# A cosine fold of w_in put ahead of the first product, and three matmuls on ones between two products, in a fused Fourier-mixing and gated-cosine kernel

## The chip, the cores and the metric

The kernel runs on one core of one Trainium2 chip. The metric is the device time of one execution in microseconds (us). The kernel before: a median of 1924.36 us in 3 runs (1923.04 to 1927.86) when the prediction was made. Each run also comes with TensorE's mean granted clock.

## The reference, cut to what matters

```python
def _attn_ref(x):                      # x: (8, 3008, 256) float32
    X = np.fft.fft(x, axis=1)
    X = np.fft.fft(X, axis=2)
    return X.real.astype(np.float32)

def _moe_ref(x, w_in, w_out):          # x: (24064, 256), w_in: (256, 2048), w_out: (2048, 256)
    h = x @ w_in
    g = h * np.cos(h)
    return (g @ w_out).astype(np.float32)
```

The second runs on the output of the first. The kernel doesn't compute the channel transform by itself: it folds the cosine and sine matrices of that transform into `w_in`, once, in its opening, and keeps the results as `Wc` and `Ws`. `w_in` comes in four quarters; a fold is a pair of matmuls for one quarter and one of the two matrices.

## The kernel before

The parts that the change touches. A fold fills a PSUM bank, and a copy on the scalar engine (ScalarE, ACT in the profile) takes it from there to `Wc` or `Ws`:

```python
def fold_mms(q, part, tag):
    ps = bank(tag)
    for h in range(2):
        mm(ps, CC[:, h * 256 + part : h * 256 + part + 128], w1[q][:, h], h == 0, h == 1)
    return ps
...
def fold_copy(q, ri):
    act((Ws if ri else Wc)[:, q * 512 : (q + 1) * 512], pending.pop((q, ri)))
```

The first spectrum's imaginary part is made from short matmuls on 95 and 94 rows into banks pB and M, a copy of pB to `ab`, and two vector ops into the ring `Ir`, both of which read bank M:

```python
def early(self, te, to):
    self.uv, self.pb = bank(te), bank(to)      # first_I: pB and M
    self.mms(0, self.uv, True)
    self.mms(1, self.pb, True)
...
def plus(self):      # Ir <- ab + M
def minus(self):     # Ir <- M - ab, the mirrored half
```

The kernel starts with matmuls on a tile of ones, to lift the clock:

```python
def warm(n):
    w = bank("M")
    for _ in range(n):
        mm(w, ones[:, 0:128], ones[:, 128:640], True)
```

Order on each engine is set by a list of pairs of a time and a function, sorted by the time (`T` is the length of a step); the times are an order, not a clock. Banks such as M exist once, so whoever takes one anew waits for its last reader.

## Time and profile before

| | before |
|---|---|
| profiled run | 1928.04 us, span (first to last instruction) 1926.1 us, mean clock 0.997 |
| TensorE busy | 99% of the span |
| first product `H<-Rr` | starts at 32.31 us, after 1.86 us of idle TensorE |
| clock at half | 32.9 to 43.1 us |
| first product of the second layer, `pA<-G` | starts at 51.35 us |

The body from there on is TensorE's nearly alone, so what counts is when TensorE gets into it. The prediction below shows the windows and TensorE's timeline. What makes the idle gap is seen in the chain that ended last, in order of time (start, duration, what):

```profile
25.53 5.66 DMA wex<-wl
...
31.27 0.48 ACT H L310
31.78 0.48 ACT H L310
32.27 0.04 issue
32.31 1.52 PE H L298 x4
```

A transfer of one row of turned weights (`wex`) takes 5.66 us, two copies into bank H follow, and the first product adds to that bank. TensorE has nothing ordered to do meanwhile.

### The profile page before, as it was taken

How to read it: one execution, taken by the hardware profiler on the slowest of the kernel's cores; microseconds unless marked ns; L12 is line 12 of the kernel's file. 1: busy time of each engine (PE TensorE's matmuls, PEld its weight loads, DVE VectorE, ACT ScalarE, POOL GpSimd, SP SyncE). 2: the span in 40 equal slices, each digit the busy share in tenths (PEclk: the TensorE clock that was granted, in tenths of full speed). 3: DMA queues.
4: the chain of work that ended last, by engine and by line, in shares of the span. 5: the costliest groups of instructions: out<-in, count | busy, mean ns of one | idle time of the engine just before them, and what ended most of it. 6: DMA issues, size and time to landing. Idle time of an engine off the chain costs nothing.

```text
span 1926.1 us, 28934 instructions
## 1 busy us (share of the span) xinstructions
PE 1908.7 (99%) x9007; PEld 1655.0 (86%) x9008; DVE 1451.3 (75%) x2364; ACT 1519.5 (79%) x2994; POOL 1521.6 (79%) x2045
## 2 busy tenths in 40 slices
PE   8999999999999999999999999999999999999998
PEld 5888888888888888888888888888888888888887
DVE  6898877777777777777777777777777777777777
ACT  3778788878878887888788787888878887877886
POOL 5788888998888888888889898888888676655554
PEclk8999999999999999999999999999999999999999
DMA  9623311322023122311232113311122110100101
GB/s 201 39 66 70 66 33 28 64 34 59 16 56 49 42 43 37 62 33 35 49 60 33 41 24 60 52 43 32 27 30 36 20 21 16 17 12 12 22 10 25
DMA packets 259969, 80.58 MB, mean 42 GB/s; under 512 B 240393, under 2 KB 243256, under 8 KB 259816
## 3 DMA queue, kind: packets, MB, share of 16 engines
q1 hardware_dynamic: 248456, 48.65, 15.5%
q0 software_dynamic: 9184, 29.83, 8.5%
q8 instruction: 72, 1.18, 0.3%
q14 instruction: 81, 0.66, 0.1%
q10 hardware_dynamic: 2176, 0.26, 0.1%
HBM read 36.72 MB, written 24.69 MB: 32 GB/s over the span
## 4 chain that ended last, share of the span: by engine, by line
PE 89%; ACT 4%; DVE 3%; issue 1%; POOL 1%; DMA 0%; POOLq 0%; DVEq 0%; ACTq 0%
PE H L298 35%; PE pC L298 16%; PE pD L298 16%; PE pB L298 15%; PE pA L298 8%; ACT G L310 1%; DVE G L840 1%; DVE G L304 1%; ACT E L310 1%; ACT z L310 1%; ACT M L310 1%; DVE v L304 1%; ACT H L310 0%; DVE M L304 0%; POOL xl L182 0%
## 5 line engine op out<-in xcount | busy, mean ns | idle before, releaser
L307 POOL TENSOR_TENSOR G<-G 128x256 f32<-128x256 f32 x1500 | 1084.4, 734 | 354.9 <-DVE G L840 278.8
L840 DVE SCALAR_TENSOR_TENSOR G<-H,G 128x512 f32<-128x512 f32 x376 | 259.1, 689 | 219.2 <-ACT G L310 218.6
L304 DVE TENSOR_TENSOR G<-H,G 128x512 f32<-128x512 f32 x376 | 259.6, 690 | 215.0 <-ACT G L310 211.7
L298 PE MATMUL H<-Ir,Ws 127*128 127x256 f32 x1504 | 388.6, 380 | 3.0 <-ACT E L310 2.3
L298 PE MATMUL H<-Rr,Wc 128*128 128x256 f32 x1504 | 388.6, 381 | 2.8 <-ACT H L310 2.8
L298 PE MATMUL pC<-G,WT 128*128 128x256 f32 x1504 | 387.5, 380 | 0.7 <-DVE u L304 0.7
L310 ACT ACTIVATE H<-Rb,wex 128x256 f32<-128x256 f32 x752 | 359.9, 479 | 24.1 <-DVE G L840 9.8
L310 ACT ACTIVATE G<-H 128x512 int32<-128x512 f32 x376 | 223.8, 595 | 179.7 <-DVE G L304 178.7
L310 ACT ACTIVATE E<-H 128x512 f32<-128x512 f32 x376 | 223.9, 595 | 163.1 <-PE H L298 161.6
L298 PEld LDWEIGHTS H<-Ir,Ws 127*128 127x128 f32 x1504 | 284.0, 190 | 47.7 <-ACT E L310 6.1
L298 PEld LDWEIGHTS pC<-G,WT 128*128 128x128 f32 x1504 | 285.2, 190 | 42.7 <-PE H L298 1.5
L298 PEld LDWEIGHTS H<-Rr,Wc 128*128 128x128 f32 x1504 | 281.3, 190 | 43.8 <-ACT H L310 5.4
L310 ACT ACTIVATE G<-G,halfpi 128x512 f32<-128x512 f32 x376 | 269.3, 716 | 2.3 <-DVE G L304 2.2
L304 DVE TENSOR_TENSOR G<-E,H 128x512 f32<-128x512 f32 x376 | 255.2, 679 | 6.1 <-PE H L298 6.1
L304 DVE TENSOR_TENSOR M<-G,M 128x512 f32<-128x512 f32 x376 | 257.6, 685 | 0.0
L840 DVE SCALAR_TENSOR_TENSOR G<-G,M 128x512 f32<-128x512 f32 x376 | 254.3, 676 | 0.5 <-ACT M L310 0.5
L310 ACT ACTIVATE M<-M,halfpi 128x512 f32<-128x512 f32 x376 | 245.6, 653 | 0.0
L298 PE MATMUL pB<-G,WT 128*128 128x256 f32 x752 | 224.7, 380 | 0.2 <-POOL G L307 0.2
L298 PE MATMUL pA<-G,w 128*128 128x256 f32 x752 | 223.9, 379 | 0.0
L310 ACT ACTIVATE M<-G 128x512 int32<-128x512 f32 x376 | 223.7, 595 | 0.0
L298 PE MATMUL pD<-G,WT 128*128 128x256 f32 x752 | 223.7, 379 | 0.0
L298 PE MATMUL pB<-G,w 128*128 128x256 f32 x752 | 223.7, 379 | 0.0
(164 smaller groups left out, 2068.3 us busy)
## 6 DMA issues: line engine op xcount, KB each, us to landing
out_dram<-ot SPq DMA_DIRECT2D x496, 32.0 KB
xl<-in_x_dram SPq DMA_DIRECT2D x64, 192.0 KB
e<-e POOLq DMA_DIRECT2D x22, 384.0 KB, 5.0
o<-o POOLq DMA_DIRECT2D x22, 381.0 KB, 4.9
out_dram<-ot SPq DMA_DIRECT2D x256, 2.0 KB
Rb<-r SPq DMA_DIRECT2D x10, 376.0 KB
w<-in_moe_w_in_dram SPq DMA_DIRECT2D x4, 512.0 KB
out_dram<-ot SPq DMA_DIRECT2D x64, 28.0 KB
```

The lines of the kernel that those rows point to most:

```text
L298: nc.tensor.matmul(out_, lhsT=lhsT, rhs=rhs, start=start, stop=stop, skip_group_check=True)
L304: pin(nc.vector.tensor_tensor(out=o, in0=a, in1=b, op=op))
L307: pin(nc.gpsimd.tensor_tensor(out=o, in0=a, in1=b, op=op))
L310: pin(nc.scalar.activation(out=o, in_=i, func=func, **kw))
L840: nc.vector.scalar_tensor_tensor(out=o, in0=h, scalar=TWO_PI, in1=c, op0=ALU.mult, op1=ALU.mult)
```

## The change

It puts a fold that doesn't depend on that transfer into the gap, moves its copy forward too, and puts three matmuls on all 128 rows of ones ahead of the second product, where TensorE waits for `Ir`. The intent is to keep TensorE's clock up.

```diff
         (0.97, first_I.copy_e),
+        (1.5, lambda: warm(3)),
         (1.0, first_I.plus),
         (1.05, first_I.minus),
-        (2.3, lambda: fold_mm(1, 0, "pD")),
+        (-0.05, lambda: fold_mm(1, 0, "pD")),
         (T + 0.5, lambda: fold_mm(2, 1)),
-        (T + 0.87, lambda: fold_copy(1, 0)),
+        (0.3, lambda: fold_copy(1, 0)),
```

## The prediction

> **What bounds the kernel now.** I read the page first (the busy shares and the clock row of the 40 slices), then the windows view over the stretches of the trace, then TensorE's timeline from 28 to 64 us, the waits, and the order of the compiled instructions with their semaphores.
>
> ```profile
> PE 1908.7 (99%) x9007; PEld 1655.0 (86%) x9008; DVE 1451.3 (75%) x2364; ACT 1519.5 (79%) x2994; POOL 1521.6 (79%) x2045
> PEclk8999999999999999999999999999999999999999
> ```
>
> TensorE is busy 99% of the span, and the windows view gives it 1796.4 of the 1800 us between 100 and 1900 us. So the body is TensorE's, and the change, which touches only the opening, can win only time by which TensorE enters the body earlier. The leading 8 of the clock row says that the clock was below full in the first 48 us slice. The windows (columns: stretch, its length, TensorE busy, granted clock, DMA share, GB/s) say where:
>
> ```profile
> 26.10:29.52 3.42, 3.42 (x22) 1.00 1.07 283
> 29.52:32.93 3.41, 1.54 (x6) 1.00 1.08 394
> 32.93:36.34 3.41, 3.41 (x15) 0.50 1.10 233
> 36.34:39.76 3.42, 2.71 (x8) 0.50 1.61 70
> 39.76:43.17 3.41, 3.41 (x6) 0.50 1.80 4
> ```
>
> The clock falls to half at about 32.9 us and comes back at about 43.1 us: 10.2 us at half speed, after a window in which TensorE was busy only 1.54 us. In the timeline:
>
> ```profile
> 28.56 1.88 PE L298 MATMUL H<-w,CC 128*128 128x512 f32 x4
> 32.31 1.52 PE L298 MATMUL H<-Rr,Wc 128*128 128x256 f32 x4 [1.86 <-ACT H L310]
> ...
> 36.53 1.52 PE L298 MATMUL M<-MC,z 94*128 94x188 f32 x4
> 38.76 2.08 PE L298 MATMUL H<-Ir,Ws 127*128 127x256 f32 x4 [0.71 <-DVE Ir L304]
> 40.62 3.14 PE L298 MATMUL pD<-w,CC 128*128 128x512 f32 x4
> 43.60 1.03 PE L298 MATMUL H<-Rr,Wc 128*128 128x256 f32 x4
> ```
>
> The reader is to see an idle gap of 1.86 us before the first product (it waits for ScalarE's copy into H, which waits for a small transfer), and that the same four-matmul group takes 1.52 and 2.08 us in the slow stretch against 1.03 us from 43.60 on, and the pD fold 3.14 us against the 1.88 us of the same form at 28.56.
>
> **What the Trainium skill says.** (1) "TensorE: Matmul & The Clock Gate", Part 1, "What's actually happening": the gate passes half or all of the pulses, decided over a free-running window of 3413 ns that doesn't restart with the kernel. The trace agrees: 32.93 to 43.1 is three such windows, and counting back from it by that window meets about 5.6 us, where the trace's first row of back-to-back opening matmuls begins to run fast (71 of them in 17.47 us). (2) The same page, "Why this matters for your kernels", allows idle gaps up to about 3 us. This trace differs: 1.86 us was enough. And 3.41 us of unbroken work on 95 rows (32.93 to 36.34) did not lift the clock, which the page doesn't mention. (3) The same page, "Architectural detail", says ScalarE and VectorE are strict FIFOs; I use that for the new place of the copy, and the timeline's order on ScalarE agrees with program order. (4) "Back-to-back issue gap" gives N/2.4 + 2.5 ns, 216 ns for 512 columns; the opening's warm bf16 matmuls took 13.26/62 = 0.214 us.
>
> **The change part by part.** The order of instructions shows three differences on TensorE and one on ScalarE; vector engine, GpSimd and the transfers keep theirs.
>
> *The fold moved forward.* Its four matmul records now stand between the fold into H at 28.56 and the first product. They need only weights that the fold before them already used. At full clock each is 0.43 us, so 1.72 us, from 30.3 to 32.0, in the gap of 1.86 us: no delay for the first product at 32.31. The window 29.52 to 32.93 is then some nine tenths busy, so the clock stays up. From 32.31: the product 0.87 us, then 16 short matmuls. The same 16 forms ran at full clock from 26.28 to 28.56, 2.28 us, so they end at 35.5 instead of 38.05. Removed from its old place, the fold saves 2.94 us (40.83 to 43.77 in the chain).
>
> *The copy moved forward.* On ScalarE it takes 0.53 us ahead of E and ab: Wc 33.93, E 34.46, ab 34.99 to 35.48. That just meets TensorE's 35.5, so the vector engine's first Ir op starts at 35.65 (38.15 before); it and the second end at 36.65.
>
> *The three matmuls on ones.* They write bank M, which the short matmuls filled and which both Ir ops read; the order shows that their weight load waits for the vector engine and that the product after them doesn't any more. So the product, which before started 0.06 us after the first Ir op, now starts after the second (+0.46 us) and after 3 x 0.214 = 0.64 us of ones: about 37.4, ending 38.4, against 38.76 and 40.83.
>
> *Sum.* H<-Ir ends 2.4 us earlier; the next H<-Rr starts at 38.3 instead of 43.77, 5.4 us earlier. But not all of that is kept. The elementwise chain starts 2.4 us earlier; ScalarE has one op (0.55 us) fewer to do there; and its wait of 1.12 us for TensorE ahead of Ws goes. Following ScalarE's queue by the durations of the rows, the copies into H for the third product end at 43.8, those for the fourth at 51.1 instead of 55.13. I take 4.1 us for the gain at this point. The wex transfer lands at 34.20 + 7.4 = 41.6, before it is wanted. From there on I see the same work shifted, and the later idle bits (1.66 us from 60 to 100) are waits between engines that shift along. Gain in the case of the profile: 4.1 us.
>
> **The rivals.** (A) *The fall of the clock is a matter of phase.* The windows run free, so whether the gap of 1.86 us falls into one window or into two differs between executions. The times before are 1923.04, 1924.36, 1927.86 and, for the profiled run, 1928.04: two pairs about 4.2 us apart, as if two had kept the clock and two had lost it, the profiled one surely having lost it. Then the change brings only the slow pair down: 1928.0 - 4.1 = 1923.9. Against the fast pair it costs: without the fall, H<-Ir would start at 36.25, so the ones and their wait add 1.1 to 1.2 us, of which the ScalarE op removed later gives back 0.55: 1923.7 + 0.6 = 1924.3. For it: the even split at the size of the gain; against it: four numbers are few, and other jitter may make them. (B) *Every run before loses the clock*, and the spread is other jitter: then the change takes 4.1 us from the median, 1920.3. (C) *The changed kernel still loses the clock.* Between 35.5 and 36.7 TensorE is idle for 1.2 us, and the 2.3 us before it are matmuls on 95 rows. If the monitor counts rows, a window around these holds about as little as the one that failed. In the trace's phase it ends at 36.34 with some 0.8 us of idle time. The clock would then halve for a window of dense work, at a loss of 1 to 2 us, in perhaps a quarter of the runs. (D) *A late transfer takes over*: the last two weight quarters or wex not landed when TensorE comes earlier. The traffic drops from 233 to 70 GB/s by 36 to 40 us, so the quarters have landed; wex has 2 us of slack. It would cost up to 2 us; I give it 5%.
>
> **Range and chances.** A at 65% gives about 1924.0, B at 25% gives 1920.3, C and D add up to 2 us to either in some runs. Weighted: 0.65 x 1924.0 + 0.25 x 1920.3 + 0.10 x 1925.5 = 1923.2. The range 1920.6 to 1925.7 leaves one tenth on each side. Two per cent is 38 us, nine times the largest effect found here, and the change adds under 2 us of work: faster 0.005, within 0.99, slower 0.005.
>
> **What would show it.** In the changed profile: pD<-w at 30.3 us within the gap; clock 1.00 from 5 us on with no half-speed stretch; pB and M groups ending near 35.5; three M<-ones at about 36.7, waiting for the vector engine's Ir; H<-Ir at about 37.4 and H<-Rr at 38.3; the first pA<-G at 46 to 47 us instead of 51.35; fast runs closer together than the 4.8 us of before. Wrong would be: a half clock again after 36 us (C); the pA group at 50 us or later, or idle stretches from 50 to 100 us that grow by as much as the opening gained; a spread as wide as before, which would deny that the clock's phase makes it.

## More of the kernel before

A step `i` of the body has two products into one bank H (`H<-Rr,Wc`, then `H<-Ir,Ws`), with a doubled copy E of the first taken between them, so the second product waits for E:

```python
def dbl(i):
    S.E = spool.tile([128, 512], FP, tag="E", bufs=2, name="E")
    act(S.E, S.H, scale=2.0)
```

## The result

| | before | after |
|---|---|---|
| median, us | 1924.22 (4 runs, 1923.04 to 1927.86) | 1924.39 (4 runs, 1924.13 to 1925.19) |
| ratio | | 0.9998, 95% interval 0.9981 to 1.0016 |
| profiled run, us | 1928.04, clock 0.997 | 1924.51, clock 0.999 |
| mean clock of the timed runs | (listed only in the later runs) | 0.999 in all four |

A ratio here is taken over the runs of both kernels, those that lost the clock (below) included, so it isn't quite the ratio of the medians. The profiled runs differ by 3.5 us, and the runs after lie within 1.1 us where those before spread over 4.8 us.

The changed kernel's page, the busy shares and the clock of the 40 slices:

```profile
PE 1905.5 (99%) x9011; PEld 1652.4 (86%) x9011; DVE 1451.9 (76%) x2364; ACT 1519.3 (79%) x2994; POOL 1522.4 (79%) x2045
...
PEclk9999999999999999999999999999999999999999
```

TensorE does one fold in another place and three matmuls more, and its busy time is 3.2 us less than before: the same work ran at full clock. The leading 8 of the clock row is now a 9. The windows of the changed kernel, cut in steps of 3.41 us counted from the first rise of its clock at 7.94 us, as all the clock windows below (stretch, length, TensorE busy, clock, DMA share, GB/s). The rise is read from the weight loads of the opening matmuls on ones, which follow each other at 0.43 us before it and at 0.21 us after it; the clock column shows 1.00 there all the same. The step is what the first profile shows: its fall at 32.93 us and its rise at 43.17 us are three steps apart and lie 8 and 11 steps after its first rise at 5.6 us, and the fall at 43.20 us in the run copy_late below lies 11 steps after its first rise at 5.7 us:

```profile
31.83:35.25 3.42, 3.42 (x22) 1.00 1.11 301
35.25:38.66 3.41, 2.24 (x11) 1.00 1.75 71
38.66:42.07 3.41, 2.16 (x7) 1.00 1.68 7
```

The clock stays at 1.00 all through the stretch that ran at 0.50 before, and the emptiest window holds 2.16 us of work. TensorE's timeline:

```profile
28.75 1.88 PE L298 MATMUL H<-w,CC 128*128 128x512 f32 x4
30.47 1.88 PE L298 MATMUL pD<-w,CC 128*128 128x512 f32 x4
32.18 1.03 PE L298 MATMUL H<-Rr,Wc 128*128 128x256 f32 x4
...
34.55 0.83 PE L298 MATMUL M<-MC,z 94*128 94x188 f32 x4
36.55 0.82 PE L298 MATMUL M<-ones 128*128 128x512 bf16 x3 [1.17 <-DVE Ir L304]
37.21 1.03 PE L298 MATMUL H<-Ir,Ws 127*128 127x256 f32 x4
38.08 1.03 PE L298 MATMUL H<-Rr,Wc 128*128 128x256 f32 x4
38.94 1.88 PE L298 MATMUL H<-w,CC 128*128 128x512 f32 x4
42.56 1.13 PE L298 MATMUL H<-Ir,Ws 127*128 127x256 f32 x4 [1.74 <-ACT E L310]
...
47.82 0.59 PE L298 MATMUL pA<-G,w 128*128 128x256 f32 x2
```

The reader is to see three things. The fold into pD fills the gap. The ones don't fill their gap: they stand after 1.17 us of idle time, released by the vector engine's second `Ir` op, and hold the product up. And a new idle time of 1.74 us stands before the second product of step 1, released by the copy E. ScalarE's timeline of the changed kernel shows why E is late:

```profile
39.49 0.59 ACT L310 ACTIVATE M<-G 128x512 int32<-128x512 f32 x1
40.72 0.72 ACT L310 ACTIVATE G<-G,halfpi 128x512 f32<-128x512 f32 x1 [0.63 <-DVE G L304]
41.35 0.64 ACT L310 ACTIVATE M<-M,halfpi 128x512 f32<-128x512 f32 x1
41.92 0.58 ACT L310 ACTIVATE E<-H 128x512 f32<-128x512 f32 x1
```

The product that E copies ended at 39.1 us; ScalarE then waits 0.63 us for the vector engine, does the two sines of step 0, and only then E. The 1.74 us belongs in part to this one execution: in the second profile of the changed kernel (after_again) ScalarE's wait is 0.27 us and TensorE's idle time 1.37 us. A vector op `e<-e,e` that goes before took 1.20 us here and 0.68 us there; why isn't shown.

### The profile page after: what moved, and what is told of

Same layout as the page of the kernel before. It is cut to its first block, busy times and chain, and to the rows that moved or that the text cites. A ratio compares the mean times of both kernels' runs of the same rounds, so it can differ in the third digit from the quotient of the medians.

```text
span 1922.5 us, 28941 instructions
## 1 busy us (share of the span) xinstructions
PE 1905.5 (99%) x9011; PEld 1652.4 (86%) x9011; DVE 1451.9 (76%) x2364; ACT 1519.3 (79%) x2994; POOL 1522.4 (79%) x2045
## 4 chain that ended last, share of the span: by engine, by line
PE 90%; ACT 4%; DVE 4%; issue 1%; POOL 0%; DVEq 0%; POOLq 0%
PE H L298 35%; PE pC L298 16%; PE pD L298 16%; PE pB L298 15%; PE pA L298 8%; ACT G L310 1%; PE M L298 1%; DVE G L840 1%; DVE G L304 1%; ACT E L310 1%; ACT z L310 1%; ACT M L310 1%; DVE v L304 1%; ACT H L310 0%; DVE M L304 0%
```

## The experiments

The theory: in the kernel before, the clock falls in some executions and not in others, by the phase of the clock's window (where its boundaries lie against the gap) and the length of the gap; the change saves the former and costs the latter about 1 us. The rivals: the fall happens every time; the ones are what keeps the clock; or moving the fold is what saves time. Twelve experiments with ten kernels were run, each on one chip (numbers 2, 7 and 4) with runs of the kernel before. All gave right results. "Lost" means that the run's mean clock is 0.998 or less, "kept" 0.999 or more: a profile with the 10 us fall has 0.997, one without 0.999 or 1.000. The split is coarse: a fall of one window takes only 0.0009 from the mean (half of 3.41 us in 1922.5), and the end of the kernel takes up to about as much (in the profile after, the last matmul ends at 1915.6 us and the clock is at half from 1919.4 us on). So a run called kept may hide a fall of one window.

Runs of one kernel still differ by 1 to 2 us with the clock kept (by 2.9 us in fold_dbl). Much of that is when the first product starts: from 31.35 to 33.16 us in the profiles, because the `wex` transfer lands at different times. So the table also has the span of the profiled run less the start of its first product, which takes that out.

| run (chip) | runs: kept / lost | mean of kept, us | mean of all, us | first product at, us | span less that, us |
|---|---|---|---|---|---|
| before | | | | 32.31 (clock lost) | 1893.8 |
| before_again (2) | 4 / 2 | 1923.1 | 1924.3 | 31.35 | 1889.6 |
| before beside the others (2) | 5 / 6 | 1923.5 | 1925.5 | | |
| fold_only (2) | 5 / 0 | 1922.9 | 1922.9 | 31.75 | 1889.1 |
| ones_only (2) | 2 / 4 | 1924.7 | 1926.8 | 32.68 | 1890.5 |
| ones_pA (2) | 5 / 0 | 1923.0 | 1923.0 | 31.98 | 1889.1 |
| before beside the others (7) | 3 / 8 | 1923.6 | 1926.6 | | |
| after | 4 / 0 | 1924.5 | 1924.5 | 32.18 | 1890.3 |
| after_again (7) | 6 / 0 | 1924.8 | 1924.8 | 31.80 | 1890.3 |
| ones_gap (7) | 6 / 0 | 1924.0 | 1924.0 | 32.23 | 1889.4 |
| copy_late (7) | 4 / 2 | 1925.3 | 1926.1 | 31.96 (clock lost) | 1892.4 |
| fold_dbl (7) | 6 / 0 | 1922.9 | 1922.9 | 32.06 | 1888.2 |
| before beside the others (4) | 4 / 5 | 1923.5 | 1925.1 | | |
| fold_only_2 (4) | 5 / 0 | 1923.4 | 1923.4 | 31.94 | 1888.9 |
| fold_dbl_2 (4) | 5 / 0 | 1923.0 | 1923.0 | 33.16 | 1888.3 |
| dbl_early (4) | 5 / 0 | 1923.7 | 1923.7 | 32.25 | 1889.2 |
| ones_gap2 (4) | 5 / 0 | 1924.1 | 1924.1 | 32.84 | 1889.6 |

Where two profiles of one kernel with the clock kept exist, the last column agrees within 0.2 us (1890.3 and 1890.3; 1889.1 and 1888.9; 1888.2 and 1888.3), so differences of half a microsecond in it can be read, though each is one profile. It isn't the sum of the waits: the two profiles of the changed kernel differ by 0.37 us in the wait for E and agree in this column. The means of five or six runs can't tell so much.

**before_again: the kernel before, no edit.**

> The kernel before, run again so that each run's mean granted clock stands beside its time. Theory (the fall of the clock is a matter of the phase of a free-running window): the runs fall into two groups, those with a mean clock near 0.997 at about 1928 us and those near 0.999 at about 1923 to 1924.5 us, with few in between, in no fixed order; the first rise of the clock in the trace stands at another time than 5.6 us from the span's start. Rival (every run loses the clock, the spread is other jitter): all runs show 0.997, whatever their time.

Measured: two groups that don't overlap. Over this kernel and the runs of the kernel before there are 37 runs: 16 kept the clock and took 1922.54 to 1924.27 us, 21 lost it and took 1925.18 to 1930.81 us. No lost run is faster than any kept one. Its profile is of a kept run; the window that holds the gap, and TensorE's timeline:

```profile
28.73:32.15 3.42, 1.66 (x6) 1.00 1.08 398
```

```profile
31.35 1.13 PE L298 MATMUL H<-Rr,Wc 128*128 128x256 f32 x4 [1.76 <-ACT H L310]
...
35.36 1.13 PE L298 MATMUL H<-Ir,Ws 127*128 127x256 f32 x4 [0.71 <-DVE Ir L304]
...
46.20 0.59 PE L298 MATMUL pA<-G,w 128*128 128x256 f32 x2
```

The same kernel reaches `pA<-G` 14.85 us after its first product here and 19.04 us after it in the first profile (51.35 - 32.31). The clock alone makes 4.2 us. The first rise of the clock stood at 4.8 us from the start here, at 5.6 us in the first profile, and between 4.8 and 7.9 us over all 14 profiles: the phase differs between executions. Rival "every run loses it" falls. One thing was not as expected: the lost runs aren't one group at 1928 us but lie from 1925.2 to 1930.8 us, and no trace of one of this kernel's shorter falls was taken. Falls of different length may make this: the one of three windows costs 4.2 us in the last column (1893.8 against 1889.6), the one of a single window in copy_late 2.1 us (1892.4 against 1890.3, a longer wait for E included).

That the phase decides is not shown. In the lost profile and in this kept one the gap lies whole in one window; what differs is its length, 1.86 and 1.76 us. And the length varies by more than that: in four profiles where something else fills the gap (ones_gap, fold_dbl, fold_dbl_2, dbl_early), 0.42 to 1.08 us of idle time remain besides 1.72 us of filler, so the empty gap would have been 2.1 to 2.8 us long (an estimate); in ones_only it was 1.58 us. The length alone could split the runs. No profile holds a gap of 1.86 us or more that a window's boundary cuts in two, which would settle it.

**fold_only: the fold and its copy moved, no ones.**

```diff
-        (1.5, lambda: warm(3)),     # against the changed kernel
```

> The fold and its copy moved as in the change, without the three matmuls on ones. Theory: the second product starts right after the first Ir op, at about 36.1 us from the start instead of 37.2, all that hangs on it comes 1.1 us earlier, the clock stays up in most runs, and the time is about 1.1 us under the changed kernel's, near 1923.3 us. Rival (the ones are needed to keep the clock): the clock falls to half in the trace after 36 us or in several of the runs (mean clock under 0.9985), and the time is 1925 us or more.

Measured: clock kept in 5 of 5 runs (and 5 of 5 again in fold_only_2), mean 1922.9 us, last column 1889.1 against 1890.3. TensorE's timeline:

```profile
34.22 0.83 PE L298 MATMUL M<-MC,z 94*128 94x188 f32 x4
35.77 1.13 PE L298 MATMUL H<-Ir,Ws 127*128 127x256 f32 x4 [0.71 <-DVE Ir L304]
...
40.85 1.13 PE L298 MATMUL H<-Ir,Ws 127*128 127x256 f32 x4 [1.37 <-ACT E L310]
```

The product waits only for the first `Ir` op (0.71 us instead of 1.17 us and the ones). The theory holds; the ones aren't needed for the clock.

**ones_only: the ones, with the fold in its old place.**

```diff
+        (1.5, lambda: warm(3)),     # against the kernel before
```

> The three matmuls on ones alone, the fold left in its old place. Theory: the idle gap of 1.9 us before the first product is back, so the clock falls in some of the runs as in the kernel before (mean clock near 0.997); and in the runs that keep it the wait for the second Ir op and the ones cost about 1.1 us against the fast runs of before, so about 1925 us with the clock kept and 1929 to 1930 us with it lost. Rival (the ones are what keeps the clock): mean clock 0.999 in all runs and a time no worse than the changed kernel's.

Measured: 4 of 6 runs lost the clock (1926.22 to 1929.01 us), the two that kept it took 1924.24 and 1925.13 us. The last column is 1890.5 against 1889.6 of the kernel before with the clock kept: the ones cost 0.9 us where 1.1 was expected. The lost runs lie below the 1929 to 1930 us expected, as the falls of the kernel before spread too. The ones don't keep the clock.

**ones_pA: the whole change, but the ones write bank pA.**

```diff
-    def warm(n):
-        w = bank("M")
+    def warm(n, tag="M"):
+        w = bank(tag)
...
-        (1.5, lambda: warm(3)),
+        (1.5, lambda: warm(3, "pA")),
```

> The whole change, but the three matmuls on ones write bank pA, which was read out long before, in place of bank M, which both Ir ops read. Theory: the ones run at about 35.4 us in the wait for the first Ir op, and the second product starts right after that op, at about 36.1 us instead of 37.2; the time is that of the run without the ones within 0.5 us and about 1.1 us under the changed kernel's. Rival (the place of the second product doesn't matter to the end, another chain sets it): the time stays at 1924.4 us.

Measured, in TensorE's timeline:

```profile
34.46 0.83 PE L298 MATMUL M<-MC,z 94*128 94x188 f32 x4
35.13 0.81 PE L298 MATMUL pA<-ones 128*128 128x512 bf16 x2
36.00 1.13 PE L298 MATMUL H<-Ir,Ws 127*128 127x256 f32 x4
```

The ones now run while TensorE would wait anyway (one of the three is missing from the trace), and the time is that of fold_only (1923.0 and 1922.9 us; 1889.1 both). So it is the bank that costs the time: in M the ones had to wait for the last reader of M, and only so did their own 0.65 us come on top.

**after_again: the changed kernel, no edit.**

> The changed kernel again, beside the others of this call. Theory (the change keeps the clock in every run and costs about 1 us in its place): every run shows a mean clock of 0.999 and a time of 1924 to 1925.2 us, which is 0.8 to 1.3 us above those runs of the kernel before that keep the clock. Rival (C of the prediction): one run in four shows 0.998 or less and is 1 to 2 us longer.

Measured: clock 0.999 or more in 6 of 6 runs, 1924.14 to 1925.53 us. With the four on record that makes ten runs without a fall that the mean clock would show, so rival C isn't seen. The second product of step 1 waits less than in the profile on record:

```profile
41.92 1.13 PE L298 MATMUL H<-Ir,Ws 127*128 127x256 f32 x4 [1.37 <-ACT E L310]
```

The mean, 1924.8 us, is 1.2 us above the kept runs of the kernel before on that chip (three runs, 1923.6 us); the profiles make it 1890.3 - 1889.6 = 0.7 us.

**ones_gap: the kernel before, with eight matmuls on ones in the gap.**

```diff
+        (-0.05, lambda: warm(8)),     # against the kernel before
         (2.3, lambda: fold_mm(1, 0, "pD")),
```

> The kernel before with eight matmuls on ones put in the idle gap before the first product, the fold left in its old place and none before the second product. Theory (filling the gap is all that matters, whatever fills it): mean clock 0.999 in every run and times like those runs of the kernel before that keep the clock, 1922.5 to 1924.1 us. Rival (taking the fold out of its old place is what wins): times 1924.4 us or more, or some runs at 0.997.

Measured: clock kept in 6 of 6 runs; last column 1889.4, as the kernel before with the clock kept (1889.6). The mean is 1924.0 us, with three of six runs above the 1924.1 us expected, by at most 0.6 us; their clocks are not lower. TensorE's timeline of the gap:

```profile
29.92 1.89 PE L298 MATMUL M<-ones 128*128 128x512 bf16 x8
32.23 1.13 PE L298 MATMUL H<-Rr,Wc 128*128 128x256 f32 x4 [0.42 <-ACT H L310]
```

So filling the gap is what saves the lost runs. Moving the fold brings, with the clock kept, only 0.3 to 0.7 us more (fold_only and its repeat against ones_gap and before_again in that column), not the 4 us.

**copy_late: the whole change, but the copy in its old place.**

```diff
-        (0.3, lambda: fold_copy(1, 0)),
+        (T + 0.87, lambda: fold_copy(1, 0)),
```

> The whole change, but the copy of the moved fold stays in its old place on the scalar engine. Theory: the copy then sits ahead of the doubled copy E of step 1, which the second product of step 1 waits for, so TensorE's idle time there grows from 1.74 us to about 2.2 us and the time by 0.3 to 0.5 us, to 1924.8 us. Rival (the copy in its new place delays the ab copy and the Ir op behind it): the time falls by up to 0.5 us.

Measured: the four kept runs have a mean of 1925.3 us, 0.5 us above after_again, as expected. What no theory expected: two of six runs lost the clock, among them the profiled one. Its windows, and TensorE's timeline:

```profile
39.79:43.20 3.41, 1.55 (x6) 1.00 1.93 4
43.20:46.62 3.42, 3.42 (x7) 0.50 1.90 3
46.62:47.00 0.38, 0.38 (x2) 1.00 1.19 2
```

```profile
42.56 1.49 PE L298 MATMUL H<-Ir,Ws 127*128 127x256 f32 x4 [1.86 <-ACT E L310]
43.84 3.26 PE L298 MATMUL pD<-w,CC 128*128 128x512 f32 x4
```

The wait for E is 1.86 us, all of it in one window, against 1.37 us in after_again on the same chip and 1.74 us in the profile on record. So the change made a second gap, which in one of its two profiles is only 0.1 us short of the one it cured; the moved copy is what keeps it short.

**ones_gap2: as ones_gap, with two ones.**

```diff
+        (-0.05, lambda: warm(2)),     # against the kernel before
```

> The kernel before with two matmuls on ones in the gap before the first product, which leave about 1.4 us of it idle. Theory (the clock falls when a window holds too little work, and the edge lies between the idle 1.74 us that the changed kernel bore ten times and the 1.86 us that fails): mean clock 0.999 in all or nearly all runs, times as in the kernel before with the clock kept. Rival (any idle time in the gap is enough in an unlucky phase): the clock falls in about half of the runs, as before.

Measured: clock kept in 5 of 5 runs. In the profiled one the transfer came late and left 1.75 us idle in spite of the ones; the window was:

```profile
29.49:32.90 3.41, 1.66 (x6) 1.00 1.07 393
```

So two windows with 1.66 us of work kept the clock (this one and that of before_again), and two with 1.54 and 1.55 us lost it. The edge lies between them as far as four profiles go. In all four the gap lies whole in one window, so they speak as well for an edge in the gap's length, between 1.76 and 1.86 us.

**fold_dbl, and fold_only_2, fold_dbl_2, dbl_early on another chip: E of step 1 ahead of the sines of step 0.**

```diff
             if i == 0:
                 dt = ahead.get(fn, dt)
+            if i == 1 and fn is dbl:
+                dt = 0.8
```

In fold_dbl and fold_dbl_2 this is done without the ones, in dbl_early with them.

> The fold and its copy moved, no ones, and E of step 1 copied ahead of the two sines of step 0. Theory (TensorE's idle time of 1.4 us ahead of the second product of step 1 is a wait for E, which sits behind the sines by order alone): the idle time goes, the first product into pA starts 0.5 to 1.4 us earlier than without that move, and the time is 0.5 to 1 us under that of the fold moved alone, near 1922 us. Rival (the copies into H for the third product, on the same engine, set the time): the idle time moves to the third product and the time stays at 1922.8 us.

> The fold and its copy moved alone, again, on the chip of the next two for comparison. Theory: 1922.8 us and a mean clock of 0.999 in every run. Rival: the earlier result was that chip's, and here the clock falls in some runs.

> The fold and its copy moved, no ones, E of step 1 ahead of the sines of step 0, again, beside the fold moved alone on the same chip. Theory: 0.5 to 1 us under the fold moved alone. Rival: the same time within 0.3 us, the idle time having only moved to later steps.

> The whole change with the ones, and E of step 1 ahead of the sines of step 0. Theory (the wait for E is the term that the prediction's sum left out): TensorE's idle time of 1.4 to 1.7 us ahead of the second product of step 1 goes, and the time falls by 0.5 to 1 us against the changed kernel, to about 1924 us, still about 1.1 us above the same kernel without the ones. Rival: the time stays at 1924.5 to 1925 us, as another wait follows.

Measured. In fold_dbl's timeline of ScalarE and TensorE:

```profile
38.99 0.59 ACT L310 ACTIVATE E<-H 128x512 f32<-128x512 f32 x1
...
39.47 0.72 ACT L310 ACTIVATE G<-G,halfpi 128x512 f32<-128x512 f32 x1
39.63 1.13 PE L298 MATMUL H<-Ir,Ws 127*128 127x256 f32 x4
```

E stands where ScalarE waited, and the idle time before the second product of step 1 is gone. `pA<-G` starts 12.84 us after the first product (44.90 - 32.06) against 14.37 us in fold_only (46.12 - 31.75), 1.5 us earlier. At the end 0.6 to 0.9 us of that is left (last column: 1888.2 and 1888.3 against 1889.1 and 1888.9), so part of it is given back to later waits: in all three profiles with E early TensorE is idle for 0.20 us before the first product of step 3, for a copy into H, which is the rival's wait. With the ones, dbl_early has 1889.2 against 1890.3: 1.1 us, just over the range expected, and it stays 0.9 us above the same without ones. The means on chip 4 are in the same order (1923.4 for the fold alone, 1923.0 with E early, 1923.7 with E early and the ones) but their differences are no larger than the spread of the runs, in which the late first product of 33.16 us takes part. So the gain of E early stands on the last column alone. One run each of fold_dbl (1925.05 us), dbl_early (1925.16) and ones_gap2 (1925.20) is far above the others of its kernel with a listed clock of 0.999 or 1.0; they stay unexplained.

The best kernel by that column is so the fold moved, no ones, E early: 0.9982 of the kernel before, lost runs included, on chip 7 (95% interval 0.9967 to 0.9996) and 0.9987 on chip 4 (0.9974 to 1.0001).

## Why the prediction was right

- **What bounds the kernel.** Right. TensorE is busy 99% of both spans, and what is won at the entry into the body stays.
- **The fold in the gap.** Right: 30.47 to 32.2 us against the 30.3 to 32.0 predicted, no delay of the first product, the clock at 1.00 from 7.9 us on. The short matmuls end at 35.40 (35.5 predicted).
- **The ones wait for bank M.** Right, in size too: they start at 36.55 (36.7), the product at 37.21 (37.4), the next one at 38.08 (38.3). ones_pA shows that the bank makes this wait.
- **The sum.** The gain over the profile before was put at 4.1 us; the spans give 3.6 us, and 3.5 us counted from the first product on. The reading of ScalarE's queue was right: the copies into H end at 43.87 and 51.17 us (43.8 and 51.1 predicted). The term that was left out is the wait of step 1's second product for E: 1.74 us of idle TensorE in the profile, 1.37 us in the second one. The prediction followed the copies into H on ScalarE's queue, where E stood in the list, but not who waited for E. So `pA<-G` starts at 47.82 us and not at the 46 to 47 us said. fold_dbl and dbl_early show that the term is real: without it the time from the first product to the end is 0.6 to 1.1 us shorter.
- **Rival A, the phase.** Right in that some runs lose the clock and others keep it, and this is the main thing: 21 of 37 runs of the kernel before lose it. That the phase is the reason is not shown, as said under before_again. It gave 1924.0 us in all; 1924.39 was measured. Its cost against the fast pair was put at 0.6 us and came out at 0.7 us by the profiles and 1.2 us by the means of chip 7. "Two groups about 4.2 us apart" was too neat: the lost runs spread over 5.6 us, and the length of the gap moves with the transfer.
- **Rival B, every run loses it.** Fallen. Its quarter of the weight is what pulled the stated 1923.2 us below A's 1924.0.
- **Rival C, the changed kernel loses it too.** Not seen in ten runs of it. It looked at the wrong place: the stretch of short matmuls was no danger (its window held 2.24 us), whereas the wait for E, which the prediction hadn't seen, lost the clock in two of six runs of copy_late.
- **Rival D, a late transfer.** Not seen: the weights were there, and in the changed kernel the products wait for E and `Ir`.

The prediction's reading that 3.41 us of work "on 95 rows" did not lift the clock is a little off: the first 0.9 us of that window are the product on 128 rows, and the last part is on 94.

So the expected gain isn't in the median because many of the runs before never paid for the fall. That the two medians agree to 0.2 us is luck of the draw: by their times three of the four runs before had kept the clock, whereas the medians of the same kernel later are 1925.63, 1926.49 and 1925.18 us. The change takes the slow runs away (the mean of all is 1926.6 us before and 1924.8 after on chip 7) and charges about 1 us to the fast ones.

## What to carry to other kernels

Ask whether a spread of a few microseconds is a state that some executions have: put the mean clock beside each run's time before comparing medians of three. A gap of TensorE near the edge (here 1.76 us kept and 1.86 us lost the clock) made a kernel of two speeds, and work that was ready, or matmuls on ones in a bank that nobody had still to read, cured it; look at which bank they write, since a bank with a late reader turned the filler into a wait. And when work is moved forward on one engine, ask for each product that now comes earlier which copy on another engine releases it, and in what order that engine does its copies.

## What the Trainium skill lacked or had wrong

- "TensorE: Matmul & The Clock Gate", "Why this matters for your kernels", allows idle gaps up to about 3 us. Here one gap of 1.86 us was enough: windows of 3.41 us with 1.54 and 1.55 us of busy TensorE lost the clock, two with 1.66 us kept it. All four gaps lay whole in one window, so these profiles don't tell a rule by the work in a window from one by the length of the gap; either way the edge lay under 1.9 us here and not near 3.
- The same page, Part 1, "What's actually happening", says that one busy window lifts the clock. In the trace of copy_late it did (43.20 to 46.62 us, matmuls on 127 and 128 rows). In that of the kernel before, the window from 32.93 to 36.34 us was 3.41 us busy, mostly with matmuls on 95 and 94 rows, and did not lift it. That the rows are the reason is a guess: no run varied them alone.
- No page says that a filler matmul must be given a bank without a late reader: bank M cost 1.2 us against pA (1890.3 and 1889.1).
